# The first pass of an attention and two-layer kernel as one computed, pinned list of parts

## The chip, the cores and the metric

One core of a Trainium2 chip. The metric is the device time of one execution in microseconds (us); less is better. PE is TensorE (PEld its weight loads), DVE is VectorE, ACT is ScalarE, POOL is GpSimd, SP is SyncE, which here only issues DMAs.

## The reference

Causal attention over 4 batches, 8 heads, 576 tokens and head size 64, mixed with a linear memory term, then two feed-forward layers over all 2304 tokens:

```python
a = softmax(causal(0.125 * q @ k.T));  local = a @ v
q_p = where(q > 0, q, exp(q) - 1) + 1
mem_out = (q_p @ M_prev) / ((q_p * z_prev).sum(-1) + 1e-6)
x = g * mem_out + (1 - g) * local              # g = sigmoid(beta), per head
x = x.transpose(0, 2, 1, 3).reshape(2304, 512)
gate = x @ w_gate                              # 512 -> 1536
x = (silu(gate) * (x @ w_val)) @ w_out         # 1536 -> 512
h = x @ w_in                                   # 512 -> 2048
out = (h * sigmoid(1.702 * h)) @ w_out2        # 2048 -> 512
```

The weights arrive as 64-bit floats, and the kernel turns them into 32-bit ones itself.

## The kernel before, in words

Tokens lie along the columns. The first pass takes the first 1024 tokens through both layers (`N1`), in two blocks of 512 columns (`COLS1`); the second pass takes the other 1280 by a scheme with seven products of half blocks (`second`). Batch 0 has tokens 0 to 575 and batch 1 has 576 to 1151, so the first block of columns needs batch 0 alone.

**Weights.** The 68 chunks of `order` (128 by 512 numbers each) are loaded as 64-bit words (`load_one`, 3 buffers), decoded in three stages (`dec_stages`: two ACT activations, three DVE operations, one POOL addition) and split into a rounded part and a rest (`split_stages`: an ACT copy, a POOL subtraction). Results go to DRAM for the second pass (`kept`); for 20 pairs of chunks, POOL adds four sums of blocks first.

**A unit** is one chunk by one block of columns: 12 matmuls into one bank of PSUM. Then ACT and DVE take the result: a tanh and a gate (`L656`, `L657`), a product with the gate (`L665`), a rounded hidden value and its rest (`L627`, `L628`), or a sum into `acc`. The first pass has 68 chunks, so 136 units.

**Attention** works on pairs of heads, 16 in all (4 a batch). For a pair, POOL scales q (`prep_q`, `L263`); the memory term goes through `phi_exp` (two activations on ACT, `L272` and `L273`), `phi_sum` (DVE, `L278`), `phi_z`, `phi_norm`, `phi_div` (POOL, `L298`), `phi_turn` (five transposes, `L304`) and `phi_out`; and four tasks k each go through `scores` (PE), `top` (a bound and a maximum, DVE), `expo` (ACT), `recip` (DVE), `norm` (POOL), `turn` (transposes, PE, `L385`, `L389`) and `turned` (ACT, `L400` to `L408`). `av` multiplies with the values and the memory (it begins with `o<-ph,mz`), and `x_hi` (`L437`) and `x_lo` (`L443`) write the layer's input.

**The order.** The first pass has three stretches. In the first (`alone`), the 8 pairs of batches 0 and 1 run by themselves, with buffers of their own (3 of qk, 6 of p, 2 of pt). Their parts, and those of the first 5 chunks (loaded once the scores of the last pair have been issued), are put in order by `ordered`: a list scheduler that books each part's engine and time, and takes on every free engine the ready part with the lowest key. `pinned` then chains each engine's instructions in that order. In the second, the units are written out in program order by the generator `moe`; `beside` gives the other 8 pairs as steps, which are put between half units in proportion to the work done, up to 93% of the pass. Nothing is pinned there. In the third, the seam, once the last chunk has been split and the last pair is done, the staging buffers make room, the stored attention output is read back (`xr`), and `halves` forms the blocks of x for the second pass (`L769` to `L785`). `halves` runs once more between the layers of the second pass.

Of the kernel before, what the change touches and what calls it, by code (L numbers as in the profile page):

```python
# [20 lines left out]
SCALE = 0.125  # L21
# [14 lines left out]
def tile_attention_moe_moe(  # L36
# [34 lines left out]
    ig = const.tile([128, 8], F32, name="ig")  # L71
    il = const.tile([128, 4, 2], F32, name="il")
# [20 lines left out]
    PASSES = B // 2  # L93
    GAP = 0.4
# [14 lines left out]
    held = {}  # L109
    bits, raws, parts = {}, {}, {}  # L110
    state = {"load": 0, "dec": 0, "split": 0, "use": 0}

    def upto(what, n, do):
        while state[what] < min(n, NCK):
            do(state[what])
            state[what] += 1

    def load_one(i):
        upto("dec", i - 2, dec_one)
# [8 lines left out]
    def dec_one(i):  # L128
        upto("split", i - 2, split_one)
        for stage in dec_stages(i):  # L130
            stage()

    def dec_stages(i):
        t = bits.pop(i)
        if not wide:
            raws[i] = t
            return [lambda: None] * 3
        top = t.rearrange("p (n t) -> p n t", t=2)[:, :, 1]
        rest = t.bitcast(U16).rearrange("p (n t) -> p n t", t=4)[:, :, 1]
        a = d3.tile([128, 512], F32, tag="wa", name="wa")  # L140
# [18 lines left out]
        raws[i] = a  # L159
        return one, two, three  # L160

    def split_one(i):
        upto("dec", i + 1, dec_one)
        for stage in split_stages(i):
            stage()

    def split_stages(i):
        wp = wpool.tile([128, 2, 512], F32R, tag="wp", name="wp")
        t = raws.pop(i)
        parts[i] = wp  # L170

        def one():
            nc.scalar.copy(wp[:, 0], t)  # L173

        def two():
            nc.gpsimd.tensor_sub(wp[:, 1], t, f(wp[:, 0]))  # L176
            if not paired[i]:
                nc.sync.dma_start(out=kept[i], in_=f(wp))
            elif i % 2 == 0:
                held[0] = t  # L180
                nc.sync.dma_start(out=kept[i][:, 0:2], in_=t.rearrange("p (a n) -> p a n", a=2))
            else:
                a1, a2 = (x.rearrange("p (a n) -> p a n", a=2) for x in (held.pop(0), t))
                m = d2.tile([128, 4, 256], F32, tag="sums", name="sums")
                nc.gpsimd.tensor_add(m[:, 2], a2[:, 0], a2[:, 1])
                nc.gpsimd.tensor_sub(m[:, 0], m[:, 2], a1[:, 0])  # L186
                nc.gpsimd.tensor_sub(m[:, 1], a1[:, 0], a2[:, 0])
                nc.gpsimd.tensor_sub(m[:, 3], a1[:, 1], m[:, 0])
                nc.sync.dma_start(out=kept[i - 1][:, 2:6], in_=m)
                nc.sync.dma_start(out=kept[i - 1][:, 6], in_=a2[:, 1])  # L190

        return one, two

    def ahead(i):
        upto("load", i + 6, load_one)
        upto("split", i + 3, split_one)
        upto("dec", i + 4, dec_one)

    def next_w():
        i = state["use"]  # L200
        state["use"] += 1
        ahead(i)
        return parts.pop(i)

    BLOCKS = (((0, 0), (1, 128)), ((2, 0),), ((3, 0),), ())
    S_COST = (0.85, 0.85, 1.06, 1.1)
    T_COST = (0.66, 0.66, 0.88, 0.55)  # L210

    def attention(pool, pairs, alone, dest):


        deep = alone
        qks, nqs, vs, es, phs, zbs, nrms = {}, {}, {}, {}, {}, {}, {}
        ss, nms, ps, sms, tps, pts, os = {}, {}, {}, {}, {}, {}, {}
        NP = len(pairs)
# [4 lines left out]
        def psum(name, score=False):  # L223
            if alone:
                return ps_a.tile([128, 2, 512], F32, tag="a", name=name)
            return ps_s.tile([128, 2, 512], F32, tag="s", name=name)

        def load_qk(i):
            if i >= NP:
                return  # L230
            b, hp = pairs[i]
            t = new("qk", [128, 2, S], 3 if deep else 2)
            for x in range(2):
                nc.sync.dma_start(out=t[:, x], in_=qk[b, hp, :, x * S:(x + 1) * S])
            qks[i] = t

        def load_nq(i):
            if i >= NP:
                return
            b, hp = pairs[i]  # L240
            if b not in zbs:
                zbs[b] = new("zb", [128, 512], 1)
                nc.sync.dma_start(out=zbs[b], in_=z[b].partition_broadcast(128))
            t = new("nq", [128, 640], 2)
            nc.sync.dma_start(out=t, in_=nat[b, hp, :, 0:640])
            nqs[i] = t

        def load_v(i):
            if i >= NP:
                return  # L250
            b, hp = pairs[i]
# [7 lines left out]
        def prep_q(i):  # L259
            if i >= NP:  # L260
                return
            t = qks[i]
            nc.gpsimd.tensor_scalar(t[:, 0], t[:, 0], SCALE, None, op0=ALU.mult)  # L263
# [4 lines left out]
        def phi_exp(i):  # L268
# [3 lines left out]
            nc.scalar.activation(e, q, AF.Relu, scale=-1.0)  # L272
            nc.scalar.activation(e, e, AF.Exp, scale=-1.0)  # L273
            es[i] = e, q

# [4 lines left out]
        def phi_z(i):  # L280
            b, hp = pairs[i]
# [4 lines left out]
        def phi_norm(i):  # L286
            hp = pairs[i][1]
# [22 lines left out]
        def scores(i, k):  # L310
            t = qks[i]
            s = ss[i, k] = psum("s", True)
# [11 lines left out]
        def top(i, k):  # L324
            s = ss[i, k]
            nm = nms[i, k] = new("nm", [128, 2, 2], 4)
            if k < 3:
                w = (384, 384, 512)[k]
                d = s[:, :, 0:w].rearrange("p j (c n) -> p j c n", n=128)
                d = d[:, :, 0:3:2] if k == 0 else d[:, :, w // 128 - 1:w // 128]  # L330
# [9 lines left out]
        def expo(i, k):  # L340
            s, nm = ss.pop((i, k)), nms.pop((i, k))
            sm = sms[i, k] = new("sm", [128, 2, 2], 4)
            p = ps[i, k] = new("p", [128, 2, 512], 6 if deep else 3)
# [12 lines left out]
        def recip(i, k):  # L356
            hp = pairs[i][1]
# [52 lines left out]
        def av(i):  # L410
# [3 lines left out]
            cut = CUTS[pairs[i][0]]  # L414
# [6 lines left out]
            for x in (1, 0):  # L421
                a, e = ends[x]
                for kc in reversed(range(4)):
                    lo = max(128 * kc, a)
                    if lo < e:
# [4 lines left out]
        def x_hi(i):  # L430
            o, b = os[i], pairs[i][0]
            parts = [(o[:, :, :NS], NS)] if CUTS[b] == NS else [(o[:, 0, :CUTS[b]], None), (o[:, 1, :S - CUTS[b]], None)]
            os[i] = []
            for (src, n), (xh, xl, done) in zip(parts, dest(*pairs[i])):
# [5 lines left out]
        def x_lo(i):  # L440
            for src, xh, xl, done in os.pop(i):
                if xl is not None:
                    nc.vector.tensor_sub(xl, src, f(xh))  # L443
                done()
# [3 lines left out]
            "load_qk load_nq load_v prep_q phi_exp phi_sum phi_z phi_norm phi_div phi_turn phi_out scores top "  # L448
            "expo recip norm turn turned av x_hi x_lo").split()}

    def beside(pool, pairs, dest):

        a = attention(pool, pairs, False, dest)
        NP = len(pairs)
        tasks = [(i, k) for i in range(NP) for k in range(4)]
        NTK = len(tasks)
        steps = []

        def add(cost, *what):
            steps.append((cost, [(a[n], args) for n, *args in what]))  # L460

        add(0.0, ("load_qk", 0), ("load_nq", 0), ("prep_q", 0), ("load_qk", 1), ("load_v", 0), ("load_nq", 1))
        add(15.0)
        for t in range(NTK + 3):
            i, k = divmod(t, 4)
            if 0 < t <= NTK:
                add(0.0, ("expo", *tasks[t - 1]))
            if 2 <= t < NTK + 2:
                add(T_COST[tasks[t - 2][1]], ("turn", *tasks[t - 2]), ("turned", *tasks[t - 2]))
            if 0 < t <= NTK:  # L470
                add(0.0, ("recip", *tasks[t - 1]), ("norm", *tasks[t - 1]))
            if t < NTK:
                add(S_COST[k], ("scores", i, k), ("top", i, k))
            if t >= 3 and tasks[t - 3][1] == 3:
                x = tasks[t - 3][0]
                add(3.9, ("av", x), ("x_hi", x), ("x_lo", x))
            if t < NTK:
                if k == 0:
                    add(0.0, ("phi_exp", i), ("phi_sum", i), ("phi_z", i))
                if k == 1:  # L480
                    add(0.0, ("phi_norm", i), ("phi_div", i))
                if k == 2:
                    add(0.7, ("phi_turn", i), ("phi_out", i), ("load_nq", i + 2))
                if k == 3:
                    add(0.0, ("load_v", i + 1), ("load_qk", i + 2), ("prep_q", i + 1))
        return steps

    def ordered(ops, stock):


        stock = dict(stock)
        left, end, order = dict(ops), {}, []
        busy, times, now = {}, [0.0], 0.0
        while left:
            for n in [n for n, t in busy.items() if t <= now]:
                del busy[n]
                for x in ops[n][5]:
                    stock[x] += 1
            used = {ops[n][0] for n in busy}
# [540 lines left out]
```

## Time and profile before

| | us |
|---|---|
| three runs: median (lowest to highest) | 1075.54 (1072.85 to 1076.27) |
| the profiled execution: its time, its span | 1074.12, 1072.3 |
| PE, DVE, POOL, ACT busy | 1020.8, 710.1, 613.5, 541.0 |
| the first matmul of a unit | at 120.75 |
| the first matmul of the second pass | at 625.76 |

The span runs from the first to the last instruction of the program; all times of rows count from its start. Matmuls are pipelined and their ends are modelled, so a PE that is shown busy is not necessarily at its full rate: the distance from one matmul's start to the next one's is the better measure.

### The profile page before, as it was taken

Reading aid. Unit: us, or ns where it says so; the run is one execution under the profiler, and the core shown is the slowest. Engines: PE = TensorE matmul, PEld = TensorE weight load, DVE = VectorE, ACT = ScalarE, POOL = GpSimd, SP = SyncE. Lnnn points to the kernel's source line nnn. Section 1 sums busy time; section 2 is a strip of 40 time slices with the busy share of each in tenths; the row PEclk is TensorE's granted clock in tenths of the full one; section 3 lists DMA queues with packets and bytes.
Section 4 is the critical chain, followed back from the end, with each engine's and each line's share of the span. In section 5 each row is a group of like instructions: output and inputs, shape, how many; then the busy total and the mean of one; then the engine's idle time right before and its main releaser. Section 6 shows DMA issues by size and latency. Waiting matters only on the chain.

```text
span 1072.3 us, 16075 instructions
## 1 busy us (share of the span) xinstructions
PE 1020.8 (95%) x5712; PEld 843.7 (79%) x5712; DVE 710.1 (66%) x1082; ACT 541.0 (50%) x1119; POOL 613.5 (57%) x634
## 2 busy tenths in 40 slices
PE   5989889999999999999999899999999999999998
PEld 2656667767777767676877789899899898989897
DVE  6887689676866778566685677247367692737373
ACT  4888645646464647574645534334135263506050
POOL 6886788875776776768374337247157051515130
PEclk8999989999999999999999999999999999999999
DMA  5333555645463635444442841221212212221202
GB/s 171 110 96 93 178 178 184 221 157 185 169 198 111 216 115 196 144 166 137 156 162 90 289 154 70 74 74 69 94 55 79 85 54 94 63 86 55 68 12 98
DMA packets 47712, 134.22 MB, mean 125 GB/s; under 512 B 7696, under 2 KB 11280, under 8 KB 47632
## 3 DMA queue, kind: packets, MB, share of 16 engines
q1 hardware_dynamic: 47488, 133.19, 37.2%
q8 instruction: 45, 0.74, 0.3%
q14 instruction: 35, 0.29, 0.1%
q10 hardware_dynamic: 144, 0.00, 0.0%
HBM read 92.80 MB, written 40.37 MB: 124 GB/s over the span
## 4 chain that ended last, share of the span: by engine, by line
PE 42%; DVE 4%; POOL 1%; issue 1%; ACT 1%; DMA 1%; SPq 0%; POOLq 0%; ACTq 0%; DVEq 0%
PE m L83 42%; DMA w<-wp 1%; DVE xl L770 1%; POOL wa L157 1%; DVE hl L628 1%; DVE tl L770 0%; PE o L83 0%; DVE ot L710 0%; ACT p L348 0%; DVE u L695 0%; POOL p L373 0%; ACT hh L627 0%; POOL sums L186 0%; DVE wa L154 0%; DMA x<-st 0%
## 5 line engine op out<-in xcount | busy, mean ns | idle before, releaser
L83 PE MATMUL m<-hh,wp 128*128 128x512 f32 (+1 forms) x1120 | 321.8, 374 | 4.2 <-DVE ot L710 3.6
L747 POOL TENSOR_TENSOR wb<-raw,wb 128x256 fp32r<-128x256 f32 x140 | 115.4, 833 | 231.8 <-ACT wb L746 227.8
L83 PEld LDWEIGHTS m<-hh,wp 128*128 128x128 f32 x1120 | 203.5, 190 | 48.5 <-issue 5.4
L83 PE MATMUL m<-xh,wp 128*128 128x512 f32 x640 | 209.1, 401 | 6.1 <-POOL wp L176 3.5
L83 PE MATMUL m<-hl,wp 128*128 128x512 f32 (+1 forms) x560 | 205.5, 373 | 2.6 <-DVE hl L628 2.5
L83 PEld LDWEIGHTS m<-xh,wp 128*128 128x128 f32 x640 | 120.6, 190 | 38.9 <-issue 6.2
L157 POOL TENSOR_TENSOR wa<-wa,wr 128x512 uint32<-128x512 uint32 x68 | 90.3, 1328 | 86.0 <-DVE wa L154 33.6
L83 PE MATMUL m<-xh,wb 128*128 128x320 f32 x640 | 127.3, 308 | 1.5 <-DVE ot L710 0.8
L83 PE MATMUL m<-xl,wp 128*128 128x512 f32 x320 | 126.8, 397 | 0.0
L83 PEld LDWEIGHTS m<-hl,wp 128*128 128x128 f32 x560 | 105.6, 190 | 24.0 <-DVE hl L628 4.6
L176 POOL TENSOR_TENSOR wp<-wa,wp 128x512 fp32r<-128x512 f32 x68 | 95.6, 1407 | 33.5 <-ACT wp L173 33.4
L83 PEld LDWEIGHTS m<-xh,wb 128*128 128x128 f32 x640 | 102.0, 187 | 2.2 <-DVE ot L710 1.3
L746 ACT CAST wb<-raw 128x256 fp32r<-128x256 f32 x140 | 56.0, 404 | 91.3 <-PE m L83 90.1
L83 PE MATMUL m<-th,wb 128*128 128x320 f32 x480 | 96.9, 309 | 0.5 <-DVE sn L814 0.5
L373 POOL TENSOR_SCALAR p<-p,sm 128x128 f32<-128x128 f32 (+3 forms) x128 | 74.6, 600 | 25.2 <-DVE sm L364 8.4
L151 DVE TENSOR_SCALAR wa<-wa 128x512 f32<-128x512 f32 x68 | 42.4, 624 | 63.7 <-ACT wa L147 63.5
L348 ACT ACTIVATE p<-s,nm 128x128 f32<-128x128 f32 (+3 forms) x128 | 65.9, 527 | 30.1 <-DVE nm L334 28.7
L148 ACT ACTIVATE wr<-w 128x512 uint32<-128x512 uint16 x68 | 46.1, 678 | 68.4 <-POOL wa L157 68.3
L83 PEld LDWEIGHTS m<-th,wb 128*128 128x128 f32 x480 | 76.8, 188 | 0.7 <-DVE sn L814 0.7
L147 ACT ACTIVATE wa<-w 128x512 f32<-128x512 f32 x68 | 45.9, 675 | 60.5 <-POOL wp L176 45.9
L83 PE MATMUL m<-xl,wb 128*128 128x320 f32 x320 | 72.7, 308 | 0.0
L628 DVE TENSOR_TENSOR hl<-u,hh 128x512 fp32r<-128x512 f32 x56 | 55.8, 999 | 24.9 <-ACT hh L627 24.4
(136 smaller groups left out, 1846.9 us busy)
## 6 DMA issues: line engine op xcount, KB each, us to landing
w<-w SPq DMA_DIRECT2D x40, 512.0 KB, 3.7
raw<-w SPq DMA_DIRECT2D x20, 896.0 KB, 4.5
w<-wo SPq DMA_DIRECT2D x28, 512.0 KB, 3.5
w<-wp SPq DMA_DIRECT2D x28, 512.0 KB, 2.6
wp<-w SPq DMA_DIRECT2D x28, 512.0 KB, 3.4
w<-sums SPq DMA_DIRECT2D x20, 512.0 KB, 3.0
qk<-qk SPq DMA_DIRECT2D x32, 288.0 KB, 4.3
nq<-nat SPq DMA_DIRECT2D x16, 320.0 KB, 3.9
```

The costliest lines, as they stand in the source:

```text
L83: nc.tensor.matmul(o, w, x, start=start, stop=stop)
L147: nc.scalar.activation(a, top.bitcast(F32), AF.Abs)
L148: nc.scalar.activation(r, rest, AF.Copy, scale=2.0 ** -13)
L151: nc.vector.tensor_scalar(a, a, HIGH, LOW, op0=ALU.min, op1=ALU.max)
L157: nc.gpsimd.tensor_tensor(au, au, r, op=ALU.add)
L176: nc.gpsimd.tensor_sub(wp[:, 1], t, f(wp[:, 0]))
L348: nc.scalar.activation(p[:, j, c:c + n], s[:, j, c:c + n], AF.Exp, bias=nm[:, x, j:j + 1], accum_out=sm[:, x, j:j + 1])
L373: nc.gpsimd.tensor_scalar(p[:, j, c:c + n], p[:, j, c:c + n], sm[:, x, j:j + 1], 1.0, op0=ALU.mult, op1=ALU.mult)
L628: nc.vector.tensor_sub(hl, u, f(hh))
L746: nc.scalar.copy(wb[:, 0], src)
L747: nc.gpsimd.tensor_sub(wb[:, 1], src, f(wb[:, 0]))
L770: nc.vector.tensor_sub(lo[:, kd], src, f(hi[:, kd]))
```

## The change

The whole first pass becomes lists of parts, each with an engine, a booked time, a key, the parts it comes after, and the buffers that it takes and gives back. A new scheduler (`schedule`) orders them, and `pinned` chains the instructions of each engine in that order, DMAs on SP too.

- **One state through the pass.** `plan_one` holds the attention of batches 0 and 1, five chunks and four units; `plan_two` holds the rest of the units, the rest of the chunks and the attention of batches 2 and 3; `seam_ops` adds the seam. The second list goes on from the engines' and buffers' times at the end of the first. The units, the decoding and the seam become parts of their own (`pe`, `tanh`, `gate1`, `val`, `hh`, `hl`, `acc_in`, `dec`, `spl0`, `spl1`, `add_up`, `keep`, `x_steps`).
- **Begun on batch 0.** The first four chunks' units on the first block of columns (`EARLY = 4`) stand in the first list, behind all attention by their keys. The first five chunks are loaded after the scores of pair 4 (`WAIT = 4`) instead of after the last pair's. The second blocks of those four chunks open the second list.
- **Booked times.** A matmul is taken as startable 0.6 us after another engine's last work for it, other engines 0.2, and after a DMA issue 4.0. Several durations differ from before, and `SHIFT` moves the keys of the attention parts of the first list.
- **Buffers.** Both stretches share one pool for attention: qk 2 (3 before in the first stretch), p 4 (6 before in the first stretch, 3 in the second), pt 1 (2 before in the first). PSUM slots are chosen by the plan. The pools of the layers are opened ahead of the attention.
- **Operations.** In batches 0 and 1 the first of the two activations of `phi_exp` becomes a minimum on POOL (`phi_neg`). `prep_q` multiplies by a number in memory and by 1.0 instead of by one constant. The two blocks of task 0 change places, so that `turned` copies them in one instruction, and `av` multiplies the first 128 columns in an instruction of its own.
- **Blocks of x.** `x_steps` forms them in the order of their use, both halves of each together, in the seam and between the layers of the second pass; the attention's output to DRAM is issued apart from `x_lo` (`x_st`).

```diff
-            nc.gpsimd.tensor_scalar(t[:, 0], t[:, 0], SCALE, None, op0=ALU.mult)
+            nc.gpsimd.tensor_scalar(t[:, 0], t[:, 0], fixed[:, 0:1], 1.0, op0=ALU.mult, op1=ALU.mult)
...
+            if i < NA:
+                nc.gpsimd.tensor_scalar(e, q, fixed[:, 1:2], 1.0, op0=ALU.min, op1=ALU.mult)
+            else:
+                nc.scalar.activation(e, q, AF.Relu, scale=-1.0)
...
-                pts[i] = new("pt", [128, 2, 1920], 2 if deep else 1)
+                pts[i] = new("pt", [128, 2, 1920], 1)
...
-                nc.scalar.copy(pt[:, :, 0:256], t[:, :, 0:256])
-                nc.scalar.copy(pt[:, :, KC + 128:KC + 256], t[:, :, 256:384])
+                nc.scalar.copy(late[:, :, 0:3, 0:128], src)
...
+    SEM, NEAR, FAR = 0.2, 0.6, 4.0
+    def schedule(ops, at):
...
+                t = max(t, tx if ex == e else tx + (FAR if ex == "SP" else NEAR if e == "PE" else SEM))
...
+                    for n in sorted((n for n in names if start[n] <= now), key=lambda n: (ops[n][2], n[0], n[1:])):
+                        if not can(n):
+                            continue
...
+    NA = 2 * HP
+    FIRST, EARLY, WAIT = 5, 4, 4
+    PACE, DEC, SHARE = 2.44, 0.0, 0.98
...
+    def plan_one():
+        ops = {}
+        for i in range(NA):
+            pair_ops(ops, i, lambda x: PACE * (4 * i + x), 1, 0)
+        for i in range(FIRST):
+            decode_ops(ops, i, PACE * 4 * NA + DEC + i, i < EARLY or i < 3)
+            e, us, key, after, *rest = ops["w", i]
+            ops["w", i] = e, us, key, (("scores", WAIT, 0),), *rest
+        for i in range(EARLY):
+            unit_ops(ops, i, 0, PACE * 4 * NA + DEC + 3.0 * i, False, "ps")
+        return ops
...
+    def plan_two(t0):
...
+        seq[:8] = [(i, c) for c in range(2) for i in range(4)]
...
+        for i in range(NA, NP):
+            pair_ops(ops, i, lambda x: t0 + dt * (4 * (i - NA) + x), 0.3, 0)
+        for n, (i, c) in enumerate(seq):
+            unit_ops(ops, i, c, t0 + per * n, ends[i] == (i, c), "m")
+        return ops, done
...
+    def pinned(ops, names, emit):
+        for n in names:
+            cur["slot"] = at["slot"].get(n)
...
+            emit[n[0]](*n[1:])
...
-    for c in moe(xh, xl):
-        spent += c
-        while steps and used < total * spent / (0.93 * MOE_T):
...
+    ops = plan_one()
+    names = schedule(ops, at)
...
+    ops, done = plan_two(max(t for e, t in at["end"].values() if e == "PE") - 6.0)
...
+    seam_ops(ops, [x[:3] for x in x_steps(None, None, "u")], done)
...
+    names = schedule(ops, at)
+    pinned(ops, names, emit)
```

## Rows read from the trace of the kernel before

**Rows 1.** The page: busy us, share of the span and instructions.

```profile
PE 1020.8 (95%) x5712; PEld 843.7 (79%) x5712; DVE 710.1 (66%) x1082; ACT 541.0 (50%) x1119; POOL 613.5 (57%) x634
```

**Rows 2.** Windows: length, busy PE, PEld, DVE, ACT, POOL, granted clock, DMA share, GB/s.

```profile
0.00:120.70 120.70, 98.77 (x704) 65.19 (x704) 90.43 (x195) 93.09 (x239) 87.83 (x131) 0.94 0.39 120
...
32.10:106.20 74.10, 69.32 (x520) 46.34 (x519) 58.54 (x127) 62.86 (x167) 54.03 (x75) 0.98 0.33 99
120.70:200.00 79.30, 72.25 (x306) 55.59 (x307) 63.72 (x89) 44.38 (x87) 67.18 (x63) 0.94 0.61 195
593.00:626.00 33.00, 28.60 (x118) 22.86 (x117) 26.82 (x36) 16.49 (x29) 9.36 (x10) 0.95 0.81 284
...
120.70:593.00 472.30, 451.63 (x2205) 343.55 (x2206) 336.77 (x534) 271.12 (x550) 333.40 (x322) 0.99 0.49 165
```

**Rows 3.** Timeline of PE at pairs 0, 6 and 7 and at the first units.

```profile
32.09 1.24 PE L83 MATMUL o<-ph,mz 128*128 128x288 f32 x4
...
106.20 1.24 PE L83 MATMUL o<-ph,mz 128*128 128x448 f32 x4
...
113.63 1.14 PE L83 MATMUL o<-ph,mz 128*128 128x448 f32 x4
...
120.75 0.50 PE L83 MATMUL m<-xh,wp 128*128 128x512 f32 x1 [1.46 <-DVE xl L443]
...
122.02 0.62 PE L83 MATMUL m<-xh,wp 128*128 128x512 f32 x2
...
124.74 0.62 PE L83 MATMUL m<-xh,wp 128*128 128x512 f32 x2
```

**Rows 4.** Timeline of the first 21 us: scores, DVE's first attention parts, transposes.

```profile
6.48 4.64 PE L83 MATMUL s<-qk 64*128 64x128 f32 x16 [6.48 <-POOL qk L263]
...
12.78 1.85 DVE L278 SCALAR_TENSOR_TENSOR phi<-nq,phi 128x640 f32<-128x640 f32 x1 [2.52 <-ACT phi L273]
14.56 0.69 DVE L332 TENSOR_TENSOR s<-s,bound 128x512 f32<-128x512 f32 x1
...
18.21 1.66 PE L83 MATMUL s<-qk 64*128 64x128 f32 x8 [5.58 <-ACT p L348]
...
18.95 1.26 POOL L298 TENSOR_TENSOR phi<-phi,nrm 128x640 f32<-128x640 f32 x1 [2.71 <-DVE sm L364]
...
20.27 1.33 PE L304 MATMUL tphi<-ident,phi 128*128 128x128 f32 x5 [0.40 <-POOL phi L298]
```

**Rows 5.** Waits of PE in 120.7:626 (27 in 13 rows): total, times, longest.

```profile
PE m L83 <- DVE ot L710: 4.4, 2, 3.6
PE o L83 <- ACT p L348: 3.6, 4, 1.7
PE m L83 <- POOL wp L176: 3.5, 1, 3.5
...
PE m L83 <- ACT hh L627: 0.2, 1, 0.2
```

**Rows 6.** Instructions of single lines: duration ns min/median/max, first and last start.

```profile
L263 POOL TENSOR_SCALAR qk<-qk x16: 1641/1650/2092, 4.8 to 472.2; 128x576 f32<-128x576 f32 x16
...
L377 POOL TENSOR_SCALAR p<-p,sm x16: 739/756/1588, 26.6 to 579.2; 128x576 f32<-128x576 f32 x16
...
L272 ACT ACTIVATE phi<-nq x16: 729/740/775, 7.9 to 464.1; 128x640 f32<-128x640 f32 x16
...
L278 DVE SCALAR_TENSOR_TENSOR phi<-nq,phi x16: 809/1223/2418, 9.4 to 467.0; 128x640 f32<-128x640 f32 x16
```

**Rows 7.** Window of the decoded chunk's tile alone: busy DVE, ACT, POOL.

```profile
120.70:626.00 505.30, 140.22 (x195) 83.69 (x131) 245.24 (x212) 0.99 0.51 173
```

**Rows 8.** Timeline of PE at the seam and between the second pass's layers.

```profile
614.82 0.73 PE L83 MATMUL m<-hh,wp 128*128 128x512 f32 x2 [3.55 <-DVE ot L710]
625.76 0.57 PE L83 MATMUL m<-xh,wb 128*128 128x320 f32 x2 [0.85 <-DVE ot L710]
868.69 0.55 PE L83 MATMUL m<-xh,wb 128*128 128x320 f32 x2 [0.62 <-DVE sn L818]
```

More of the change, by code (lines that the diff above doesn't have):

```diff
@@ L108, in tile_attention_moe_moe, with load_w @@
             if not paired[i] or i % 2 == 0 else None for i in range(NCK)]
[L109 to L119, printed above, removed]
+    bits, raws, parts, sums, stages = {}, {}, {}, {}, {}
+    def load_w(i):
         if wide:
@@ L194, in ahead, with dec @@
[L194 to L215, printed above, removed]
+    def dec(i, x):
+        if x == 0:
+            stages[i] = dec_stages(i)
+        stages[i][x]()
@@ new lines, in keep @@
+    def keep(i):
+        if not paired[i]:
+            nc.sync.dma_start(out=kept[i], in_=f(parts[i]))
+        elif i % 2 == 0:
+            nc.sync.dma_start(out=kept[i][:, 0:2], in_=raws[i].rearrange("p (a n) -> p a n", a=2))
+        else:
+            nc.sync.dma_start(out=kept[i - 1][:, 2:6], in_=sums.pop(i))
+            nc.sync.dma_start(out=kept[i - 1][:, 6], in_=raws[i][:, 256:512])
+    BLOCKS = (((1, 0), (0, 256)), ((2, 0),), ((3, 0),), ())
+    NP = B * HP
+    at = {"fifo": {}, "slots": {}, "end": {}, "free": {}, "slot": {}}
@@ L235, in load_qk, with load_z @@
             qks[i] = t
+        def load_z(b):
+            zbs[b] = new("zb", [128, 512], 1)
+            nc.sync.dma_start(out=zbs[b], in_=z[b].partition_broadcast(128))
         def load_nq(i):
[L238 to L243, printed above, removed]
+            b, hp = divmod(i, HP)
             t = new("nq", [128, 640], 2)
@@ L356, in recip @@
         def recip(i, k):
-            hp = pairs[i][1]
+            hp = i % HP
             if k < 3:
@@ L447, in attention @@
         return {n: names[n] for n in (
[L448 to L485, printed above, removed]
-        return steps
@@ L488, in ordered @@
[L488 to L499, printed above, removed]
-            ready = sorted(
-                (key, n) for n, (e, us, key, after, takes, gives, do) in left.items()
-                if all(x in end and end[x] + (LAG.get(ops[x][0], 0.2) if ops[x][0] != e else 0.0) <= now for x in after))
-            for key, n in ready:
-                e, us, _, _, takes, _, _ = ops[n]
-                if e in used or any(stock[x] < 1 for x in takes):
-                    continue
-                for x in takes:
-                    stock[x] -= 1
-                used.add(e)
-                del left[n]
-                order.append(n)
-                end[n] = busy[n] = now + us
-                times += [now + us, now + us + 0.2, now + us + LAG.get(e, 0.2)]
-            times = sorted({t for t in times if t > now})
-            assert times or not left, sorted(left)
-            now = times[0] if times else now
-        return order, now
@@ new lines, in plan_one, with seam_ops @@
+    def plan_one():
[9 more added lines that the diff above has]
+        return ops
+    def seam_ops(ops, steps, done):
+        before = tuple(n for n in ops if n[0] in ("x_st", "sum", "spl1") or n[0] == "keep" and paired[n[1]])
+        ops["seam",] = "SP", 0.8, done - 60.0, before, (), ()
+        free = "pe", NCK - 5, 1, 1
+        for n, (e, name, after) in enumerate(steps):
+            us = {"SP": 0.4, "DVE": 0.95, "Act": 0.8}[e]
+            needs = [("x", m) for m in after]
+            if e == "SP":
+                needs.append(("seam",))
+            elif name[0] == "B" or name == "T1":
+                needs.append(free)
+            ops["x", n] = e, us, done - 22.0 + 0.5 * n, tuple(needs), (), ()
+        for n in range(2):
+            ops["raw", n] = "SP", 0.4, done - 22.0 + 2 * n, (("seam",),), (), ()
+        for n in range(7):
+            ops["mk", n] = "Pool", 0.85, done - 14.0 + n, (("raw", 0),), (), ()
@@ new lines, in hl, with acc_in @@
+    def hl(i, c):
+        hi, lo = (x[:, slice(*COLS1[c])] for x in HS[i])
+        nc.vector.tensor_sub(lo, U[i, c], f(hi))
+    def acc_in(i, c):
+        two, at_, ins, g = layer(i)
+        if two not in ACC:
+            ACC[two] = accs.tile([128, 4, N1], F32, tag="acc", name="acc")
+        ac, o = ACC[two][:, at_ - ins, slice(*COLS1[c])], T[i, c]
+        if g == 0:
+            if two:
+                nc.scalar.activation(ac, o, AF.Copy, scale=0.5)
+            else:
+                nc.scalar.copy(ac, o)
+        elif not two:
+            nc.vector.tensor_add(ac, ac, o)
+        else:
+            if g == 3:
+                U[i, c] = new_u()
+            nc.vector.scalar_tensor_tensor(U[i, c] if g == 3 else ac, o, 0.5, ac, op0=ALU.mult, op1=ALU.add)
```

667 lines of the change are left out of this document (377 added, 290 removed).

## The prediction

> **What bounds the kernel now.** The page comes first. PE is shown busy for 95% of the span and no other engine for more than 66% [rows 1], so time is to be won where PE stands still or runs below its clock. The windows say where that is [rows 2]. Before the first unit at 120.75 us [rows 3], PE is idle for 120.70 - 98.77 = 21.9 us; from there to 593 for 472.30 - 451.63 = 20.7; in the seam, 593 to 626, for 33.00 - 28.60 = 4.4. After 626 comes the second pass, which the change leaves as it is but for the order of its blocks of x between two layers. The granted clock is 0.94 in 0:120.70 and in 120.70:200 and 0.95 in the seam, so that parts of these ran at 1.2 GHz and not at 2.4; over all of 120.7:593 it is 0.99.
>
> Is PE also the bound of the first stretch? From `av` of pair 0 at 32.09 to `av` of pair 6 at 106.20 are 74.11 us, 12.35 a pair [rows 3]. Of these PE is busy for 69.32 us, ACT for 62.86, DVE for 58.54, POOL for 54.03 [rows 2]: 11.6, 10.5, 9.8 and 9.0 us a pair. PE comes first, and all four are near each other. So early units don't find a free PE there; they fill what little is idle, and the stretch gives back its idle time and no more.
>
> The idle time is worst at the start. PE issues the first scores at 6.48 us; DVE takes them up at 14.56 only, since in its order the second `phi_sum` stands ahead, waits 2.52 us for ACT and takes 1.85 itself. All PSUM tiles are then full, and PE waits 5.58 us, to 18.21 [rows 4]. In the middle stretch and the seam PE stops 27 times, for 26.2 us in all, and every other engine ends some of these waits: no single line is at fault [rows 5].
>
> **How much is work in the middle.** Four groups of three matmuls make a unit, and one unit's length is 124.74 - 122.02 = 2.72 us [rows 3]; 136 units are 370 us. The stretch and the seam last 505.3 [rows 7]; without 25.1 of idle time and 370 of units, 110 us are left for 8 pairs, 13.8 each, more than the 11.6 above, since the clock's loss and the changes between kinds of matmul are in it. The Trainium skill ("Perfetto Trace Analysis", section "Identifying the Most-Contended Engine") warns that a matmul's busy share says little about headroom and looks at the weight loads' share instead. By it, PEld's 343.55 of 472.30 us [rows 2] would leave 129 us, and the kernel could come down to some 947. I go by the starts of the units, which follow each other at the same distance whatever the busy share is, and give that case 1 in 100, within C below.
>
> **The change part by part.** *First stretch.* PE's busy time there stays 98.8 us and the four early units add 10.9, which the middle stretch then lacks: the same work, which before ended at 120.75 + 10.9 = 131.6. What counts is PE's idle time. 6.5 us of it lie before the first scores. A further 5 to 6 are the way of the first pair from scores to transposes, from 14.56 to 20.27 [rows 4]. The new plan books 4.0 us for a load and so takes the bound of pair 0's scores ahead of `phi_sum`; that moves this way forward by up to 5 us. Later gaps can be filled by units once chunks are decoded, after pair 4's scores. I take 12.5 us of idle time in place of 21.9: **-9.4**. Bounds: 0, if units only displace attention and the shallower buffers (one pt, two qk) cost what the better start gives; -15.4, if only the first 6.5 us stay.
>
> Could another engine be in the way? ACT loses the Relu, 0.74 us a pair [rows 6]: 9.7. DVE has 9.8 a pair, five chunks at 140.22 x 3 / 195 = 2.16 us [rows 7], and six takings of units of under 1 us: 78 + 11 + 6 = 95 us, from 9.4 on. POOL gains `phi_neg` on 640 columns, which no row shows; its form is that of `L377` (0.756 for 576 columns), so 0.84, with 1.83 as the upper bound from `L263` (1.650 for 576) and nothing as the lower one, which a pass over 640 columns excludes. `prep_q` takes the form of `L377` and falls from 1.65 to 0.76. So POOL stays at 9.0 a pair, 72 us; on the tiles of 65 chunks it spends 245.24 us [rows 7], 3.8 each with splits and sums, so 19 for five: 91 us. PE's 109.7 are above all of them. The single copy for task 0 and the extra `av` instruction I take at nothing, as the columns moved are the same; they hide in ACT's free time and, on PE, cost at most a tenth of a us a pair, 1.6 in all.
>
> The clock, 0.94 over 120.7 us, is worth at most 7.2 us; much of that lies in idle time. I take **-1.5**.
>
> *Middle stretch.* With the units as parts, one stands ready at nearly every moment, so PE should stop only where a planned part comes late. There are 80 attention parts on PE (ten a pair, 8 pairs). The plan books 0.6 us before a matmul; the trace shows 20.27 - (18.95 + 1.26) = 0.06 [rows 4], so 0.54 is margin, and half units of 1.36 us add to it. Against it, `phi_sum` is booked at 0.95 and takes 1.223 in the median and 2.418 at worst [rows 6]; DVE is free for 135 of 472 us [rows 2] and can catch up. I take 0.1 us a part, 8 us: **-12.7**, with bounds of -20.7 (no wait) and 0 (as many as now). The loads and stores on SP are pinned too: a store that waits for POOL holds the loads behind it, but by the keys these stand 23 us ahead of use. The 3.5 us for a split chunk [rows 5] should go, as the second blocks of four decoded chunks open this stretch. The clock's 6% of 79.3 us is at most 4.8; I take half, **-2.4**.
>
> *Seam.* PE waits for DVE in two places, 3.55 and 0.85 us [rows 8], where DVE forms blocks and takes up units in turn. In order of use, the first product needs one block's two halves alone. I take 1 us left: **-3.4**, bounds 0 and -4.4. Between the second pass's layers the same order could save the wait of 0.62 or cost as much, as spare tiles are held longer: 0.
>
> Sum: 9.4 + 1.5 + 12.7 + 2.4 + 3.4 = 29.4 us. The profiled execution took 1074.1 (span 1072.3): 1044.7. The median of the runs lies 1.4 above it, and so I put the forecast at **1046 us**.
>
> **The rivals.** *A: one half works.* If the static order stops PE in the middle as often as the loose one did, 15.1 us fall away: 1061. If all engines being near their bound eats the first stretch's gain, 10.9 fall away: 1057. For it: the waits now are many and small [rows 5], which is what errors of booked times look like. Against: the margin of 0.54 us.
>
> *B: slower, as pinned parts come late.* The place is the 80 attention parts on PE in the middle stretch, each ahead of units that could run. If `norm` or `turned` is late, PE waits with work at hand. The price: 26.2 us in 27 waits is 0.97 each now; 80 such waits are 78 us in place of 20.7, so with the other gains of 14.3 (first stretch and seam, no clock) the time is 1075.5 - 14.3 + 57.3 = 1118. It decides from (20.7 + 14.3) / 80 = 0.44 us a part on average. Against it: PE's own delay gives DVE and POOL, idle for 29%, time to come in front again. The Trainium skill's "TensorE: Matmul & The Clock Gate" has, in its opening table, strictly ordered queues for ACT, DVE and POOL; by that a late part there holds up all behind it, which is B's way on. No row here shows the contrary.
>
> *C: more than forecast.* The bounds of all terms, 15.4 + 7.2 + 20.7 + 4.8 + 4.4 = 52.5, give 1023.
>
> **How the numbers follow.** Forecast (1033 to 1056): 0.54. A (1056 to 1068): 0.18. C (below 1033): 0.12. B: 0.11 for slower by more than 0.3%, and 0.05 for waits that just eat the gain. 0.3%, 3.2 us, is about what a measurement tells from no change. For 8 in 10, B and the ends of A and C are left out: 1027 to 1064. Faster 0.84, same 0.05, slower 0.11.
>
> **What would show it.** DVE's first bound at 9 to 10 us instead of 14.56; the first `m<-xh,wp` at 75 to 100, ahead of pair 7's `av`; `L263` at 0.76; PE idle for 6 to 12 us from the end of that `av` to the seam, and 0 to 2 in it; the first `m<-xh,wb` at 594 to 600 instead of 625.76, and from there to the end the same 446.5 us. I am wrong if the first idle time stays near 22 us, if waits for `p`, `pt` or `hl` on PE add up to over 20, or if the units start at another distance than 2.72.

## The result, and the profile after

The changed kernel takes 1059.64 us (median of 4 runs, 1059.06 to 1060.18); the kernel before, in 4 runs beside it, 1074.19 (1072.61 to 1076.27). The ratio is 0.9863, with a 95% interval of 0.9842 to 0.9885. The profiled execution took 1059.94 us, its span 1058.1. The time is 13.6 us above the forecast of 1046: inside the range of 1027 to 1064, but in the band of rival A (1056 to 1068) and not in the forecast's own (1033 to 1056).

For the comparison the span is cut at three matmuls of units, counted by their starts in the trace: the 49th (48 matmuls, the work of four units, are done), the 1537th, with which the last eight units begin, and the first of the second pass.

| us | to the 49th | to the 1537th | to the second pass | second pass | span |
|---|---|---|---|---|---|
| before | 131.8 | 465.7 | 28.3 | 446.6 | 1072.3 |
| after | 135.8 | 443.6 | 30.2 | 448.5 | 1058.1 |
| difference | +4.0 | -22.1 | +1.9 | +1.9 | -14.2 |
| forecast | -10.9 | -15.1 | -3.4 | 0 | -29.4 |

The middle stretch brought more than forecast; the three others each cost time. The line of busy times of the changed kernel's page answers to [rows 1]:

```profile
PE 1015.0 (96%) x5776; PEld 851.5 (80%) x5776; DVE 731.6 (69%) x1084; ACT 534.8 (51%) x1095; POOL 633.8 (60%) x642
```

The windows of the changed kernel, with the columns of [rows 2], in order of time:

```profile
0.00:135.80 135.80, 110.95 (x784) 77.91 (x785) 98.14 (x207) 91.76 (x232) 115.33 (x151) 0.94 0.37 116
...
30.90:103.00 72.10, 62.82 (x454) 42.66 (x453) 57.97 (x119) 55.12 (x140) 68.03 (x81) 0.93 0.43 134
135.80:579.40 443.60, 438.04 (x2210) 341.39 (x2208) 355.25 (x529) 269.80 (x538) 325.69 (x311) 0.99 0.52 173
...
601.40:609.60 8.20, 0.04 (x1) 0.00 (x0) 8.20 (x13) 2.65 (x4) 0.00 (x0) 0.81 0.72 293
609.60:613.00 3.40, 3.37 (x13) 3.40 (x14) 3.40 (x5) 1.45 (x2) 0.00 (x0) 0.50 0.22 82
```

And of the kernel before, cut at the same points:

```profile
0.00:131.80 131.80, 109.82 (x753) 74.34 (x754) 95.74 (x204) 97.96 (x248) 95.08 (x138) 0.95 0.41 127
...
131.80:597.50 465.70, 445.08 (x2177) 338.12 (x2176) 334.26 (x528) 268.52 (x545) 327.45 (x316) 0.99 0.49 165
```

*First stretch.* PE's idle time rose from 131.80 - 109.82 = 22.0 us to 135.80 - 110.95 = 24.9. Between the first `av` and 103 us the engine with the most work is no longer PE: POOL is busy for 68.03 of 72.10 us (94%), PE for 62.82 (87%); before, PE was busy for 94% there [rows 2]. The lines say which instruction did it; durations are minimum, median and maximum, as in [rows 6]:

```profile
L236 POOL TENSOR_SCALAR phi<-nq,fixed x8: 2418/2422/2423, 9.9 to 88.0; 128x640 f32<-128x640 f32 x8
...
  ACT phi L243: 17.3, 5
```

That is `phi_neg`: 2.42 us where the prediction put 0.84 and had 1.83 as its upper bound. ACT waited for it 5 times, 17.3 us in all. The timeline of ACT and PE at the start shows what this did:

```profile
12.34 0.74 ACT L243 ACTIVATE phi<-phi 128x640 f32<-128x640 f32 x1 [6.86 <-POOL phi L236]
16.65 0.74 ACT L243 ACTIVATE phi<-phi 128x640 f32<-128x640 f32 x1 [3.58 <-POOL phi L236]
17.29 0.46 ACT L317 ACTIVATE p<-s,nm 128x256 f32<-128x256 f32 x1
...
19.10 2.93 PE L84 MATMUL s<-qk 64*128 64x256 f32 x12 [8.02 <-POOL nq L253]
```

DVE takes up pair 0's scores at 7.60 us (14.56 before [rows 4]), as the plan meant. But in ACT's pinned order the second pair's exponential of the memory term stands ahead of the first exponential of the scores; it waits for the second minimum, and ACT gets to the scores at 17.29 us only. PE then stands for 8.02 us, where it stood for 5.58.

*Middle stretch.* PE's idle time fell from 465.70 - 445.08 = 20.6 us to 443.60 - 438.04 = 5.6. The waits of PE in 135:590 fill three rows; before, in 131.80:597.50, they fill eleven:

```profile
PE s L84 <- DVE phi L247: 3.4, 1, 3.4
PE tp L354 <- POOL p L342: 1.8, 3, 1.2
PE m L84 <- DVE hl L802: 0.2, 1, 0.2
```

*Seam.* PE's last matmul of a unit starts at 601.05 us; the first of the second pass starts 8.6 us later. DVE's timeline, with that matmul of PE's at the end:

```profile
603.85 0.68 DVE L819 SCALAR_TENSOR_TENSOR u<-m,acc 128x512 f32<-128x512 f32 x1
604.45 0.81 DVE L681 TENSOR_TENSOR tl<-t,th 128x640 fp32r<-128x640 f32 x1
605.18 0.81 DVE L681 TENSOR_TENSOR tl<-xr,th 128x640 fp32r<-128x640 f32 x1
605.91 0.81 DVE L690 TENSOR_TENSOR t<-t 128x640 f32<-128x640 f32 x1
606.65 1.55 DVE L681 TENSOR_TENSOR xl<-t,xh 128x640 fp32r<-128x640 f32 x2
608.12 0.81 DVE L681 TENSOR_TENSOR tl<-t,th 128x640 fp32r<-128x640 f32 x1
608.86 0.68 DVE L819 SCALAR_TENSOR_TENSOR u<-m,acc 128x512 f32<-128x512 f32 x1
...
609.63 0.87 PE L84 MATMUL m<-xh,wb 128*128 128x320 f32 x2 [8.19 <-issue]
```

The last taking of a unit (608.86) stands behind six steps that form blocks of x, although its matmuls ended soon after 601; PE starts 0.09 us after it ends. DVE is busy for all 8.20 us of the pause, so in the pause nothing is late: this says that the order itself makes PE wait, and e8 below tests it. The Trainium skill's "TensorE: Matmul & The Clock Gate" (opening table) has VectorE's queue as strictly first in, first out; this row agrees, with 7.8 us between the last matmul's start and its taking. After the pause the granted clock is 0.50 for 3.40 us, TensorE's lower level of 1.2 GHz; by estimate that is 3.40 x 0.50 = 1.7 of the second pass's extra 1.9 us.

### The profile page after: what moved, and what is told of

The parts are those of the page before. It is cut to its first block, busy times and chain, and to the rows that moved or that the text cites. A ratio compares the mean times of both kernels' runs of the same rounds, so it can differ in the third digit from the quotient of the medians.

```text
span 1058.1 us, 16144 instructions
## 1 busy us (share of the span) xinstructions
PE 1015.0 (96%) x5776; PEld 851.5 (80%) x5776; DVE 731.6 (69%) x1084; ACT 534.8 (51%) x1095; POOL 633.8 (60%) x642
## 4 chain that ended last, share of the span: by engine, by line
PE 78%; DVE 11%; POOL 4%; DMA 4%; issue 2%; ACT 1%; SPq 1%; POOLq 0%; DVEq 0%; ACTq 0%
PE m L84 67%; PE s L84 4%; PE o L84 4%; PE tp L354 2%; DVE wa L138 1%; DVE wa L139 1%; POOL p L342 1%; DVE wa L136 1%; DVE hl L802 1%; DVE sm L333 1%; DMA out<-u 1%; POOL phi L236 1%; DVE nm L303 1%; DMA nq<-nat 1%; PE tp L358 1%
## 5 line engine op out<-in xcount | busy, mean ns | idle before, releaser
L861 POOL TENSOR_TENSOR wb<-raw,wb 128x256 fp32r<-128x256 f32 x140 | 118.8, 856 | 232.0 <-ACT wb L860 229.2
L84 PE MATMUL m<-xh,wp 128*128 128x512 f32 x640 | 212.8, 401 | 0.0
L142 POOL TENSOR_TENSOR wa<-wa,wr 128x512 uint32<-128x512 uint32 x68 | 96.8, 1425 | 56.7 <-DVE wa L139 33.6
L342 POOL TENSOR_SCALAR p<-p,sm 128x256 f32<-128x256 f32 (+3 forms) x128 | 79.5, 638 | 17.5 <-DVE sm L334 10.6
L317 ACT ACTIVATE p<-s,nm 128x256 f32<-128x256 f32 (+3 forms) x128 | 66.1, 531 | 19.8 <-DVE nm L303 18.3
L84 PE MATMUL s<-qk 64*128 64x256 f32 (+3 forms) x256 | 51.4, 512 | 21.4 <-POOL nq L253 8.0
L84 PEld LDWEIGHTS m<-xl,wp 128*128 128x128 f32 x320 | 60.7, 190 | 11.6
L802 DVE TENSOR_TENSOR hl<-u,hh 128x512 fp32r<-128x512 f32 x56 | 56.4, 1016 | 10.9 <-ACT hh L798 10.4
L139 DVE SCALAR_TENSOR_TENSOR wa<-w,wa 128x512 uint32<-128x512 uint32 x68 | 62.2, 915 | 2.3
```

The costliest lines, as they stand in the source:

```text
L84: nc.tensor.matmul(o, w, x, start=start, stop=stop)
L139: nc.vector.scalar_tensor_tensor(au, top, 0xC0000000, au, op0=ALU.bitwise_and, op1=ALU.bitwise_or)
L142: nc.gpsimd.tensor_tensor(au, au, r, op=ALU.add)
L317: nc.scalar.activation(p[:, j, c:c + n], s[:, j, c:c + n], AF.Exp, bias=nm[:, x, j:j + 1], accum_out=sm[:, x, j:j + 1])
L342: nc.gpsimd.tensor_scalar(p[:, j, c:c + n], p[:, j, c:c + n], sm[:, x, j:j + 1], 1.0, op0=ALU.mult, op1=ALU.mult)
L802: nc.vector.tensor_sub(lo, U[i, c], f(hi))
```

## The experiments

Ten kernels ran, all edits of the changed kernel. The table has their stretches, cut as above in the profiled execution, and their times (e2_forms and e7_near ran once). The kernel before, run beside them, took 1074.66 us (beside e1, e2, e3 and e6), 1072.35 (e5, e8, e9, e13) and 1074.02 (e7, e14), so a difference of some 2 us between times of different groups is not clear of the noise.

| us | to the 49th | to the 1537th | to the second pass | second pass | time |
|---|---|---|---|---|---|
| after | 135.8 | 443.6 | 30.2 | 448.5 | 1059.64 |
| e1_relu_act | 130.0 | 449.5 | 30.6 | 449.2 | 1059.83 |
| e2_forms | 128.4 | 442.7 | 30.2 | 448.8 | 1051.83 |
| e9_product | 124.6 | 442.7 | 29.9 | 449.4 | 1048.69 |
| e13_relu_same_order | 125.6 | 443.8 | 30.6 | 448.8 | 1050.07 |
| e3_seam_late | 135.4 | 444.6 | 31.2 | 448.1 | 1061.20 |
| e8_takings_first | 136.5 | 443.2 | 25.1 | 450.7 | 1056.95 |
| e5_early0 | 139.3 | 439.3 | 35.5 | 448.1 | 1066.63 |
| e6_loose | 143.8 | 450.2 | 37.4 | 448.5 | 1081.89 |
| e7_near | 134.1 | 449.3 | 30.6 | 448.3 | 1064.13 |
| e14_relu_takings | 124.7 | 444.2 | 26.2 | 451.1 | 1047.02 |

### The minimum on POOL

The theory: POOL's minimum, 2.42 us eight times, made POOL the bound of the first stretch. The rival: the pinned order or the shallower buffers did it, and the minimum only fills time that POOL has. First the operation goes back to ACT, and the plan books it there:

```diff
-            op("phi_neg", -0.5, (i,), *(("Pool", 1.0) if alone else ("Act", 0.74)), (("load_nq", i),), ("e",))
+            op("phi_neg", -0.5, (i,), "Act", 0.74, (("load_nq", i),), ("e",))
...
-                nc.gpsimd.tensor_scalar(e, q, fixed[:, 1:2], 1.0, op0=ALU.min, op1=ALU.mult)
+            nc.scalar.activation(e, q, AF.Relu, scale=-1.0)
```

> The minimum on POOL (phi_neg) goes back to ACT as a Relu for batches 0 and 1, and the plan books it there; all else stays. Theory P: phi_neg, 2.42 us on POOL where 1.0 was booked, makes POOL the bound of the first stretch (busy 68.03 of 72.10 us) and holds ACT's first exponential back to 17.29 us. Then POOL falls by 2.4 us a pair, the first exponential of scores starts before 13 us, the 49th matmul of the units starts at 124 to 128 us instead of 135.8, and the time is 1047 to 1052. Rival Q: the shallower buffers (one pt, two qk, four p) and the units among the attention hold the first stretch; then the 49th matmul stays within 3 us of 135.8 and the time at 1057 to 1061.

1059.83 us (1058.12 to 1061.07), ratio to before 0.986 (0.9839 to 0.9881): a miss, no faster than the change. The first stretch did shorten by 5.8 us (to 130.0, not to 124 to 128), but the plan, computed again with the other booking, gave another order, and its middle stretch was 5.9 us longer. So this run can't decide: it changes two things.

Next, four forms of the same instruction, in turn over the eight pairs: with the number in memory on a flat view of the tile, a product in its place, the minimum with a constant in one operation, and the product on the flat view.

```diff
+                if i % 4 == 0:
+                    nc.gpsimd.tensor_scalar(e2, q2, fixed[:, 1:2], 1.0, op0=ALU.min, op1=ALU.mult)
+                elif i % 4 == 1:
+                    nc.gpsimd.tensor_scalar(e, q, fixed[:, 0:1], 1.0, op0=ALU.mult, op1=ALU.mult)
+                elif i % 4 == 2:
+                    nc.gpsimd.tensor_scalar(e, q, 0.0, None, op0=ALU.min)
+                else:
+                    nc.gpsimd.tensor_scalar(e2, q2, fixed[:, 0:1], 1.0, op0=ALU.mult, op1=ALU.mult)
```

> Four forms of phi_neg side by side, on pairs 0 to 7 in turn: (0) minimum with a number in memory on a flat 128x640 view, (1) a product with a number in memory on the four-dimensional view, (2) minimum with a constant in the instruction on the four-dimensional view, (3) a product with a number in memory on the flat view. The output of pairs with a product is not that of the reference, as the minimum is left out there. If the operation is what is slow, forms 0 and 2 take about 2.4 us, 1 and 3 about 0.84. If the view is slow, 1 and 2 take 2.4, and 0 and 3 about 0.84.

The lines of the four forms:

```profile
L238 POOL TENSOR_SCALAR phi<-nq,fixed x2: 2422/2424/2425, 9.8 to 51.3; 128x640 f32<-128x640 f32 x2
L240 POOL TENSOR_SCALAR phi<-nq,fixed x2: 792/794/797, 14.1 to 55.3; 128x640 f32<-128x640 f32 x2
L242 POOL TENSOR_SCALAR phi<-nq x2: 1807/1810/1814, 32.3 to 74.1; 128x640 f32<-128x640 f32 x2
L244 POOL TENSOR_SCALAR phi<-nq,fixed x2: 792/795/798, 39.6 to 81.9; 128x640 f32<-128x640 f32 x2
```

The view makes no difference, and in this form the operation does: 0.79 us for a product of the very form and size that takes 2.42 as a minimum. With one constant and no second operation it is otherwise: the minimum takes 1.81, and the product of the kernel before, 1.650 for 576 columns [rows 6], would take 1.83 for 640 by an estimate that goes by columns. So minima are not slow and products fast in every form; it is the instruction with a number in memory and two products that is fast. The "GPSIMD Engine Reference" of the Trainium skill (section "4.1 Engine selection") calls one-input work on GpSimd roughly line-rate. The instructions with two products, at 0.79 us next to the 0.80 of VectorE's reduction over a tile of that size (`L258`), agree with it; the minima at 1.81 and 2.42 us don't. POOL lost 4 x 1.63 + 2 x 0.61 = 7.7 us of work, and the first stretch 7.4.

To leave the order alone, the next two keep the plan as it is and change the instruction only: e9 puts the product in place of all eight minima, e13 issues the Relu on ACT at the places that the plan gave the minima.

```diff
-                nc.gpsimd.tensor_scalar(e, q, fixed[:, 1:2], 1.0, op0=ALU.min, op1=ALU.mult)
+                nc.gpsimd.tensor_scalar(e, q, fixed[:, 1:2], 1.0, op0=ALU.mult, op1=ALU.mult)
```

> phi_neg of batches 0 and 1 becomes a product with a number in memory (0.79 us in the side-by-side run, where the minimum took 2.42); the minimum is left out, so the memory term of these pairs is not the reference's. Plan and order are those of the changed kernel to the instruction. Theory P: POOL's time bounds the first stretch, so of 8 x 1.63 = 13 us most comes back: the 49th matmul of the units at 123 to 126 us instead of 135.8, and the time 1046 to 1051. Rival Q (buffers and units hold the stretch; the 8 us of the side-by-side run came from elsewhere): 1055 to 1060.

> The Relu of batches 0 and 1 is on ACT as before the change, but every part keeps its place in the computed order, for which it stays booked on POOL. If the run with the Relu on ACT and a new plan lost its 5.8 us again because the new plan happened to order the middle stretch worse, here the first stretch gains 6 to 11 us and the middle keeps its length (443.6 us from the 49th matmul to the 1537th), so 1049 to 1054. If ACT's 0.74 us a pair cost as much as POOL's 2.42, the time stays at 1058 to 1061.

e9: 1048.69 us (1047.82 to 1049.88), ratio 0.9776 (0.9761 to 0.9791). e13: 1050.07 us (1048.81 to 1050.65), ratio 0.9787 (0.9772 to 0.9801). The window 30.90:103.00 of e13, which answers to the changed kernel's 62.82 for PE and 68.03 for POOL:

```profile
30.90:103.00 72.10, 65.97 (x507) 44.74 (x504) 61.58 (x124) 63.51 (x161) 60.52 (x82) 1.00 0.42 131
```

PE is first again, and its clock is 1.00 instead of 0.93. With 0, 7.7 and 8 x 1.62 = 13.0 us taken from POOL, the first stretch lasts 135.8, 128.4 and 124.6 us: 7.4 come back for the first 7.7 and 3.8 for the next 5.3. In e13 another 6.4 us leave POOL and ACT gains 8 x 0.74 = 5.9, and the stretch is no shorter (125.6): POOL alone no longer bounds it. The rival falls for these 10 to 11 us, since order and buffers are the same in all four; whether the shallower buffers hold some of the idle time that is left, no run tests. In e13 ACT reaches pair 0's first exponential at 12.85 us, not 17.29. The first stretches of e1 and e13 differ in order alone, and so do their middles: 443.8 us against 449.5.

### The seam

Two ways to get the last takings out from behind the x steps. The first books 9 us, not 4, for the reads of the attention output, so that the plan itself would put those steps later:

```diff
-                t = max(t, tx if ex == e else tx + (FAR if ex == "SP" else NEAR if e == "PE" else SEM))
+                t = max(t, tx if ex == e else tx + ((9.0 if x[0] == "x" else FAR) if ex == "SP" else NEAR if e == "PE" else SEM))
```

> The plan books 9.0 us instead of 4.0 for the loads of x in the seam, and so puts DVE's steps on them later among the takings of the last units; no operation changes. Theory S: in the seam the last taking of a unit (608.86 us on DVE) stands in the pinned order behind steps on x whose data come late, and PE waits for its bank until 609.63. Then PE's gap before the second pass falls from 8.2 us to under 3, the clock there stays at its upper level, and the time falls by 5 to 9 us, to 1051 to 1055. Rival: DVE's work in the seam, busy without a pause from 601.4 to 609.6, is the bound wherever it stands; then PE stops within the first seven products for as long, and the time falls by under 2 us.

A miss: 1061.20 us (1059.27 to 1061.42), ratio 0.9874 (0.9856 to 0.9892), not to be told from the change. The last taking came at 610.40 us, still the last of DVE's steps ahead of the second pass, and PE started at 611.19. The second moves them by hand:

```diff
+    a, b = names.index(("acc", NCK - 2, 1)), names.index(("acc", NCK - 1, 1))
+    late = [n for n in names[a:b] if n[0] == "x"]
+    names = [n for n in names[:b + 1] if n not in late] + late + names[b + 1:]
```

> In the seam alone: DVE's and ACT's steps on x that stand between the takings of the last three units are put behind the last taking; the rest of the order is unchanged. Theory S: PE waits for the last taking, whose place in DVE's order sets the start of the second pass. Then the second pass starts 4 to 7 us earlier (603 to 606 instead of 609.63) and some of it is lost again where T2 and T3 come later; the time falls by 3 to 7 us, to 1053 to 1057. Rival: DVE's work in the seam is the bound in any order; then PE's waits move into the first seven products and the time falls by under 1.5 us.

1056.95 us (1056.49 to 1057.3), ratio 0.9851 (0.9834 to 0.9867). DVE and PE at the seam of this kernel:

```profile
601.37 1.40 DVE L819 SCALAR_TENSOR_TENSOR u<-m,acc 128x512 f32<-128x512 f32 x2
604.00 0.69 DVE L819 SCALAR_TENSOR_TENSOR u<-m,acc 128x512 f32<-128x512 f32 x1 [1.23 <-DMA out<-u]
...
604.79 0.78 PE L84 MATMUL m<-xh,wb 128*128 128x320 f32 x2 [3.03 <-issue]
```

The seam shrinks by 5.1 us with the same operations: that the order made the wait is shown. 2.2 us come back as a longer second pass, 1.2 of them as waits of PE for DVE, whose steps now come later; and of the pause that is left 1.23 us is a new wait, for the store of an earlier output to free its buffer `u`. The pause of 3.03 us is followed by the low clock as well (the last section has the row). What is won on the whole is small: the medians differ by 2.7 us, the ratios to the kernel before by 1.3, and their intervals overlap.

### What the parts are worth

`EARLY` from 4 to 0 takes the early units out:

> No units in the first list (EARLY = 0); chunks are still loaded after pair 4's scores, and all 136 units stand in the second list. If the early units fill idle time of PE, the 49th matmul comes 4 to 9 us later than 135.8 and the time is 1063 to 1069. If they only displace attention in a stretch that POOL bounds, pair 7's `av` comes earlier by as much, and the time stays within 3 us of 1060.

1066.63 us (1064.03 to 1066.88), ratio 0.9937 (0.9921 to 0.9953): the plan without early units is 7.0 us slower, as the first theory had it. In the traced execution, the fastest of its four, it is 4.1: the 49th matmul comes 3.5 us later, a little less than expected, the seam grows by 5.3 and the middle shrinks by 4.3. As the early units also shape the plan of what follows, this run doesn't show what they are worth by themselves.

The second list issued in the planned order, with its instructions not chained to each other:

```diff
-    pinned(ops, names, emit)
+    pinned(ops, names, emit, False)
```

> The second list is emitted in the computed order, but its instructions are not chained; the toolchain may move them, as it could before. If the pinning is what took the waits out of the middle stretch, PE's idle time between the first list's end and the seam returns from 5.6 to 12 to 20 us and the time is 1067 to 1075. If the computed order alone does it, PE stays idle for under 8 us there and the time within 3 us of 1060.

1081.89 us (1080.0 to 1082.33), ratio to before 1.0067 (1.0048 to 1.0086): 22 us slower than the change and slower than before, beyond the expected 1067 to 1075. The middle stretch:

```profile
143.80:594.00 450.20, 436.82 (x2174) 336.90 (x2172) 312.48 (x516) 263.56 (x530) 304.44 (x299) 1.00 0.48 160
```

PE is idle for 450.20 - 436.82 = 13.4 us, against 5.6 pinned. So the gain hangs on the chain too, and not on the order of issue alone. This stretch holds 6.6 of the 22 us. The seam is 7.2 longer, and the 49th matmul comes 8.0 later, although the first list is pinned as before: POOL is busy for 126.39 us up to it, not 115.33.

The margin ahead of a matmul, on which the prediction rested its 8 us:

```diff
-    SEM, NEAR, FAR = 0.2, 0.6, 4.0
+    SEM, NEAR, FAR = 0.2, 0.06, 4.0
```

> The changed kernel with the planner's margin between a producer's and a reader's booking cut from 0.6 to 0.06 us; the plan is computed again, so the order of the lists changes too. If the margin is what keeps TensorE from waiting in the middle, its idle time between the 49th unit product and the eighth before the last rises from 5.6 us to over 10 us, as it was before the change (20.6 us). If the pinned order by itself does it, the idle time stays under 8 us.

One run: 1064.13 us, and an idle time of PE in the middle of 449.30 - 439.29 = 10.0 us. That is the margin theory's number, but it doesn't decide: e1, with the full margin and another order, has 449.50 - 440.41 = 9.1. What the margin does can't be told here from what any other order does.

### Both costs taken away

The edits of e13 and e8 together:

> The changed kernel with two edits together: the memory feature's negative part by ScalarE's Relu again, emitted in the place that the plan gave GpSimd's minimum (the order of the list is unchanged), and the ten weight-decoding steps between the last three units' takings put behind the last taking. If GpSimd's minimum sets the first stretch and the steps ahead of the last taking set the seam, and neither touches the other, their savings against the changed kernel add: 9.6 us and 2.7 us, so 1046 to 1049 us, with the 49th unit product at 125 to 126 us and a seam of 25 to 26 us. If the seam's gain is given back by what the moved steps delay in the second pass, the time is that of the first edit alone, 1049 to 1051 us.

1047.02 us (1045.43 to 1048.3, 5 runs), ratio to before 0.9743 (0.973 to 0.9756), the fastest version. What the second edit moves are the steps on x, as in e8, and not steps of weight decoding, as the expectation has it. The two savings, 9.6 and 2.7 us, would add to 1047.4, so they add up within the noise. PE starts the second pass at 595.04 us.

## Why the prediction came out as it did

**Direction and range held; the forecast failed in the first stretch.** The prediction's own sign of being wrong, a first idle time that stays near 22 us, came: it was 24.9. The step that failed is "its form is that of `L377` (0.756 for 576 columns), so 0.84": the price of a minimum was read from a product. It is 2.42 us, above the upper bound of 1.83 too, which was also a product's. The next step, POOL at 91 us with PE's 109.7 above it, fell too: POOL is busy for 115.33 us to the 49th matmul, above PE's 110.95, which was forecast well. But the price alone makes it only 91 + 8 x 1.58 = 104. Most of the other 12 us lies in "POOL stays at 9.0 a pair": the window of that figure, 32.10:106.20 before, holds `prep_q` only four times for its six pairs, and 44 of 48 instructions of `norm`'s first three tasks (the row has the count, busy us, mean ns and idle us before):

```profile
L263 POOL TENSOR_SCALAR qk<-qk 128x576 f32<-128x576 f32 x4 | 6.6, 1648 | 0.0
```

Over the whole first stretch before, POOL's attention lines take 80.4 us for eight pairs, 10.0 each. Neither error by itself would have put POOL above PE; the two together did. Taken away with the order kept, the minimum returns 135.8 - 125.6 = 10.2 of the 14.9 us by which this stretch missed. The rest: idle time that doesn't go as low as 12.5 us. In e13 125.6 us hold 108.59 of PE's work, so 17.0 idle, 10.9 of them in the first 30.9 us (20.01 busy); what keeps it there stays open. `prep_q` was right: 0.75 us in the median, 0.76 forecast.

**The start of the first stretch was half right.** DVE's first bound was forecast at 9 to 10 us and came at 7.60. But "that moves this way forward by up to 5 us" looked at DVE alone; what was late next was ACT, behind the minimum. The first unit, forecast at 75 to 100 us, came at 111.80.

**The middle stretch was right in its direction, and larger.** "0.1 us a part, 8 us" of idle time was 5.6 in 5 waits; 12.7 forecast, 15.0 measured. The clock, forecast at 2.4, gave about 1.7: it was 0.50 for 6.7 us from 155.2 and for 3.3 from 189.3 before, and is 0.50 for 6.7 from 162.8 now, so (10.0 - 6.7) x 0.50. These two make 16.7 of the 22.1 us; the other 5.4 lie in PE's busy time. About as much shows where PE changes between units and attention: without waits, the matmuls at such changes take 37.1 us from start to start before (152 changes) and 31.5 now (144). Why each change is shorter stays open. The margin as the reason of the few waits stays open as well.

**The seam was wrong.** "In order of use, the first product needs one block's two halves alone" looked at the first product's input and not at its PSUM, which waits for the takings of the last units; those stand in the same pinned queue. 3.4 gained was forecast, 1.9 lost, and 1.9 more in the second pass. With the takings in front (e8) the seam is 3.2 us shorter than before, close to the forecast; but the second pass then is 4.1 longer, so that against the kernel before nothing is won there.

**The rivals.** A's second form, "all engines being near their bound eats the first stretch's gain", with its 1057, is nearest to what came, and the time lies in A's band; but it didn't name the engine or the instruction. B didn't happen: 5.6 us over 80 parts is 0.07 a part, far from its 0.44. (Its gain of 14.3 holds the clock's 1.5 us, though the sum says "no clock"; without them B decides from 0.42 and costs 1120, which changes nothing.) C's bound of the middle, 20.7 + 4.8, was nearly reached (22.1), but the other stretches took it back. That e14 lands 1.0 us from the forecast is partly luck, the sum of errors of both signs, the larger middle against the first stretch's idle time and the longer second pass.

## What to carry to other kernels

Price an instruction that is moved to another engine by a row of that very operation on that engine, and where none exists, give the bound room and check what a wrong price would make the bound. Before a window's busy time is divided by the pairs in it, count each instruction in it: prefetched work can stand outside. In a computed, pinned order one wrong price is paid twice, by the engine and by all that stands behind it in the chains; when a price is corrected, change the instruction with the order held first, since a new plan alone moved the middle stretch by 6 us. At the end of a pinned stretch look for the work that frees the next stretch's resources, not only for that which makes its input.

## What the runs showed of the hardware

On POOL, with 128 by 640 32-bit floats, a minimum with a number in memory followed by a product with 1.0 takes 2.42 us and two products in one instruction 0.79, each on both views; a minimum with a constant alone takes 1.81. A product with a constant alone took 1.65 on 128 by 576 [rows 6], where the instruction with a number in memory and two products takes 0.75. Which of its two differences makes it faster, the number in memory or the second product, no run separates.

A pause of PE of 8.2 us at the seam was followed by 3.4 us at a granted clock of 0.50. Shorter pauses did the same: one of 3.03 us in e8 (0.51, first row below), and one of 3.55 us before the first pass's end in the kernel before [rows 8], after which the clock was 0.50 in 616.00:619.30. After the wait of 0.85 us ahead of its second pass [rows 8] the kernel before ran at 1.00 (second row):

```profile
604.79:608.20 3.41, 3.41 (x13) 3.41 (x14) 3.35 (x5) 1.45 (x2) 0.00 (x0) 0.51 0.98 389
...
625.80:629.20 3.40, 3.40 (x23) 3.40 (x24) 0.64 (x1) 1.00 (x2) 0.24 (x1) 1.00 0.93 276
```
